# Three output chunks at once in the first batch's second layer, and the weight loads of the next batch at its end

## The chip, the cores and the metric

The kernel runs on one core of one Trainium2 chip. The metric is device time in microseconds (us) of one execution. The core has five engines that run their own instruction lists side by side and wait for each other by semaphores: TensorE (PE in the profile; PEld is its weight load), VectorE (DVE), ScalarE (ACT), GpSimd (POOL), and SyncE (SP), which here only issues DMA transfers.

## The reference

Eight batches of attention with normed queries and keys, then a two-layer block over all 3584 rows:

```python
q_n = q / sqrt(mean(q*q, -1) + 1e-6) * g_q        # q, k, v: (8, 12, 448, 64), float32
k_n = k / sqrt(mean(k*k, -1) + 1e-6) * g_k
attn = softmax(q_n @ k_n.T / sqrt(64)) @ v        # softmax over the keys
x = attn.transpose(0, 2, 1, 3).reshape(8 * 448, 768)
h = x @ w_in                                      # w_in: (768, 2048)
out = ((h - tanh(h)) @ w_out).astype(float32)     # w_out: (2048, 768)
```

`w_in` and `w_out` come in as float64, two 32-bit words for each number; the kernel rounds them to float32 itself.

## The kernel before

**Attention** is cut into 48 steps, one for each batch and pair of heads (numbered `s`; six steps to a batch). Each step's q and k blocks (`qk_nat`) and v block (`v_nat`) are loaded by SP, the squares are summed and turned into a factor `rr`, q and k are multiplied by it, transposed on TensorE (L467, L471), multiplied to scores (L569), put through the exponential on ScalarE (L575), and multiplied with v (L635, L623, L677). The sums for the softmax are products with ones (L700, in `totals`), and `totals` takes their reciprocal on VectorE (L705). Results of TensorE lie in banks of two pools: `sc` with five banks for attention and `mm` with three for the two layers; each pool is handed out in turn, so a bank is free again only when its last reader is done. For two steps (s = 11 and 12, in `visit`) `totals` takes a bank of `mm`.

**The two layers** are written as a Python generator, `mlp()`. It yields after each matmul, and the attention slots draw so many of them between their own parts. So the two kinds of work are interleaved in one list on TensorE, in an order fixed when the program is built. For the first two batches the generator gives, in order, `hidden(0)`, `project_first(0)`, `hidden(1)`, `project(1)`.

- `hidden(b)` is the first layer of batch b by a scheme of seven products in place of eight: four sets (`j` = 0 to 3) of seven products `p`, in the order 1, 5, 6, 2, 3, 7, 4. A product is 12 matmul records at L857 and takes about 2.27 us. After a product, `use(p, bank)` takes it from its bank: a copy by ScalarE for p=1 (L924), sums by VectorE for p=5, 6, 7, 3, 4 (L926, L928, L932 and L933, L936, L940), a tanh and a difference for p=2 (`shrink`, L904 and L905); the other differences are queued in `late["todo"]` and come some products later, on GpSimd. The three `mm` banks take turns, with p=2, 3 and 7 added into the banks of 1, 5 and 6.
- `project_first(0)` is the plain second layer of batch 0: six output chunks of 128 columns, each a chain of 16 matmuls (`f` = 0 to 15) of 448 columns at L1339, one chunk after the other (the right half of `w_out` first). At a chunk's end ScalarE copies the bank (L1345), and `store` transposes it on VectorE (L966) and queues its four DMAs (L971) in `late["out"]`, which `step_out` issues later.

**The weights** come in 32 pieces, 0 to 15 of `w_in` and 16 to 31 of `w_out`. A piece is loaded raw by SP (`weight_load`), and rounded in three stages: ScalarE (L71, L72), VectorE (L78, L79, L82), GpSimd (L92). Three raw buffers serve all pieces from the eighth on, and `place_free` lets a load be issued only when the piece three before it is through. `weight(to)` rounds pieces up to number `to`. In `hidden(0)` the list `due` gives `to` for each of the 28 products; in `project_first` a formula in `m` does, for the first three chunks. Four pieces of `w_in` make the eight operands of one set, by sums of VectorE in `combine` (L357), and `keep_step` writes the seven that are needed to a scratch tensor in DRAM (L388) for the later batches.

**The ring.** After `w_in` is used, its memory is a ring of six places (`SLOTS`), handed out in turn by `ring_slot`. `combine_w_out(f)` (L381 to L384) puts sums of `w_out` in two places, from where `keep_factors` writes them to DRAM; the DMAs wait in `late["keep"]` until the next such step. Then the ring serves `ring_load(to)`: it loads the operands of the next batches' layers up to number `to` from DRAM by SP (L427 in the first layer). `hidden(1)` uses one such load of 384 KB for each product.

In `project_first` the order before is, by matmul number `m` from 0 to 95:

| m | what is put in the lists ahead of the matmul |
|---|---|
| 0 to 47 | `weight(...)`, 8 pieces in all |
| 48, 49 | the last two pieces of `w_out` to DRAM |
| 52, 56, ... 80 | `combine_w_out(0)` to `(7)`, with the DMAs of the one before |
| 84 | two ring loads, then the last DMAs of `w_out` |
| 86 | two more ring loads |
| each chunk's middle | the stores of the chunk before (two `step_out`) |

The other ring loads are issued in `hidden(1)`, where places come free. In `hidden(1)` the attention slot also loads `qk_nat` in a changed form (L497): its squares are summed by ScalarE (L501, tile `sum_T`) and VectorE (L508, tile `rr_mine`), between the sums of the products in VectorE's list.

SP issues all DMAs of the kernel in one list, in the order in which the program was written. The framework puts in the semaphore waits.

Of the kernel before, what the change touches and what calls it, by code (L numbers as in the profile page):

```python
# [147 lines left out]
def bounded_path(tc, ctx, q, k, v, moe_w_in, moe_w_out, out, g_col, ident, ones, half_ones, neg_half, early):  # L148
# [66 lines left out]
    def mm_bank():  # L215
        return bank_of("mm")
# [170 lines left out]
    def keep_factors(n, count, f, src):  # L387
        nc.sync.dma_start(  # L388
# [28 lines left out]
            ring_steps += [(first, 2, p, part) for p in outer for part in (1, 2, 3, 4, 0)]  # L417
    ring_tiles = {}

    def ring_load(to):  # L420

        for n in range(len(ring_tiles), min(to, len(ring_steps))):
            b, layer, j, p = ring_steps[n]
            t = ring_tiles[ring_steps[n]] = ring_slot()
            if layer == 0:
                assert kept[1] > j
                nc.sync.dma_start(out=t[:, : 2 * HALF], in_=w_in_dram[j, p])  # L427
            elif layer == 2 and p == 0:
                nc.sync.dma_start(out=t, in_=w_out_dram[:, BLOCKS[j], HC - 1].rearrange("p f d -> p (f d)"))
            elif layer == 2:  # L430
                n = min(2 * HB, 7 * HB - 2 * (p - 1) * HB)
                at = 2 * (p - 1) * HB
                nc.sync.dma_start(out=t[:, :n], in_=inner_dram[j][:, at : at + n])
            else:
                nc.sync.dma_start(out=t, in_=w_out_dram[:, BLOCKS[p], j].rearrange("p f d -> p (f d)"))


    normed, turned, probs, sums, whole, xT, tt = {}, {}, {}, {}, {}, {}, {}
# [208 lines left out]
    def visit(s, av):  # L647

        wave(*half_values(s, 2, av, True))
        for c in range(2):  # L650
            v0, v1 = half_values(s, c, av, False)
            if has(s + 1):
                (s0, exp0), (s1, exp1) = scores(s + 1, c, True)
                wave(s0, v1)
                exp0()
                wave(v0, s1)
                exp1()
            else:
# [158 lines left out]
    assert len(due) == 7 * SETS and due[-1] == CF + HF  # L817

    def part(name):
        if name == "th" and "blocks" in late:  # L820
# [60 lines left out]
    def hidden(b):  # L881

        if b < PAIRED or b % 2 == 0:
            g = gp.tile([P, CF, S], F32, name="gT")
        else:
            g = late["second"].tile([P, CF, S], F32, name="g2")
        late["g"] = g
        if b >= PAIRED:
            late.setdefault("us", {})
            late["pair_g"] = [g, None] if b % 2 == 0 else [late["pair_g"][0], g]  # L890
        single = b and b < PAIRED
        t2 = late["tg"].tile([P, 3, HF, HS], F32, name="tg") if single else None
        late["t"] = t2
        x = [xT.pop((b, c)) for c in range(CD)]
        t = [tt.pop((b, i)) for i in (0, 1, 3)]
        low, high = slice(0, HS), slice(HS, S)
        moving = {
            1: lambda c: x[c][:, low], 2: lambda c: x[c + HC][:, low], 3: lambda c: x[c + HC][:, high],
            4: lambda c: t[2][:, c], 5: lambda c: t[0][:, c], 6: lambda c: t[1][:, c], 7: lambda c: x[c][:, high],
        }  # L900

        def shrink(rows, cols, h, eng):
            th = part("th")
            nc.scalar.activation(th, h, AF.Tanh, bias=0.0, scale=1.0)  # L904
            eng.tensor_tensor(out=g[:, rows, cols], in0=h, in1=th, op=ALU.subtract)  # L905

        def done_with(j):
            up, down = slice(2 * j, 2 * j + 2), slice(HF + 2 * j, HF + 2 * j + 2)
            s1, s2, s5 = part("s1"), part("s2"), part("s5")

            def factors():

                g11, g12, _, g22 = (g[:, r, c] for r in (up, down) for c in (low, high))
                f1, f2 = (t2[:, i, up] for i in range(2))
                nc.vector.tensor_tensor(out=f1, in0=g12, in1=g11, op=ALU.subtract)
                nc.vector.tensor_tensor(out=f2, in0=g22, in1=f1, op=ALU.subtract)
                nc.gpsimd.tensor_tensor(out=g12, in0=g22, in1=g12, op=ALU.subtract)

            def use(p, bank):
                v = view(bank)  # L920
                if b >= PAIRED:
                    beside_hidden(b, j, p)
                if p == 1:
                    nc.scalar.copy(out=s1, in_=v)  # L924
                elif p == 5:
                    nc.vector.tensor_tensor(out=s5, in0=v, in1=s1, op=ALU.add)  # L926
                elif p == 6:
                    nc.vector.tensor_tensor(out=s2, in0=v, in1=s1, op=ALU.add)  # L928
                elif p == 2:
                    shrink(up, low, v, nc.vector)  # L930
                elif p == 7:
                    nc.vector.tensor_tensor(out=s5, in0=v, in1=s5, op=ALU.add)  # L932
                    nc.vector.tensor_tensor(out=s1, in0=v, in1=s1, op=ALU.add)  # L933
# [375 lines left out]
    def project_first(b):  # L1309
# [4 lines left out]
        late["todo"] = []  # L1314
        keep_step(0, SETS - 1)
        took = 4 * S / ENGINE_NS
        for m in range(CD * CF):
            k, f = m // CF, m % CF
            n = (k + HC) % CD
            if f == 0:  # L1320
                bank = mm_bank()
            if f == CF // 2:
                step_out(2)
            if k < HC:
                weight(CF + HF + HF * (m + 1) // (HC * CF))
            elif m < HC * CF + 2:
                keep_w_out(PIECES - 2 + m - HC * CF)
            elif (m - HC * CF) % 4 == 0 and m - HC * CF <= 4 * HF:
                for fn in late["keep"]:
                    fn()  # L1330
                late["keep"] = []
                combine_w_out((m - HC * CF) // 4 - 1)
            elif m == CD * CF - 12:
                ring_load(2)
                for fn in late["keep"]:
                    fn()
            elif m == CD * CF - 10:
                ring_load(4)
            nc.tensor.matmul(  # L1339
                bank[:, :S], lhsT=w_out_row(f, n // HC)[:, n % HC * P : (n % HC + 1) * P], rhs=g[:, f, :],  # L1340
                start=(f == 0), stop=(f == CF - 1),
            )
            if f == CF - 1:
                y = part("s2").rearrange("p f s -> p (f s)")
                nc.scalar.copy(out=y, in_=bank[:, :S])  # L1345
                store(b, n, y)
            yield took
        wp_stack.close()
        late["blocks"] = pool("blocks", bufs=1)
# [530 lines left out]
```

## Time and profile before

Three runs took 1344.74, 1344.65 and 1343.43 us, median 1344.65. The profiled execution is one more run.

| what | value |
|---|---|
| profiled execution, whole | 1342.53 us |
| its span, from first to last instruction | 1340.70 us |
| mean granted clock of TensorE | 0.998 of full |
| ScalarE / VectorE / GpSimd busy | 42% / 72% / 59% |
| `project_first(0)`, L1339, from first to last matmul | 176.25 to 268.5 us, with attention between |
| first record of `hidden(1)` | 274.46 us |

How to read it: one line of a timeline is one instruction or a run of like ones: start, length, engine, source line, operation, tiles written and read, and in brackets how long the engine had been idle before it and what ended that (the engine, tile and line whose result came last). TensorE's matmuls overlap, so a run of records is read by its start and end, not by adding their lengths. The names `w_f`, `w_out` and `w_in` of tiles are the ring (as operands of `w_in` and later loads), the rounded `w_out`, and the scratch in DRAM.

### The profile page before, as it was taken

To read this page: it belongs to the slowest core of one execution; us is meant where nothing else is said; L and a number is where in the kernel's file an instruction comes from. 1 tells how busy PE (TensorE), PEld (TensorE's weight loads), DVE (VectorE), ACT (ScalarE), POOL (GpSimd) and SP (SyncE) were. 2 spreads that over 40 slices of the span, in tenths; PEclk is the share of its full clock that TensorE was granted. 3 is DMA by queue.
4 is the path that set the end of the run, shared out by engine and by line. 5 is a ranking of instruction groups with operands and counts; after the bars stand their busy time and mean duration, and the time that the engine had idled before them with its cause. 6 is when DMAs were issued, how large, how long until landed. Compare 5 with 4: busy or idle time off the path is not lost.

```text
span 1340.7 us, 29301 instructions
## 1 busy us (share of the span) xinstructions
PE 1311.5 (98%) x11368; PEld 1033.4 (77%) x11368; DVE 969.5 (72%) x1410; ACT 568.1 (42%) x1328; POOL 795.0 (59%) x591
## 2 busy tenths in 40 slices
PE   7989999999999999999999999999999999999997
PEld 3467854488998888688878788779887888799986
DVE  4999978867765767688888576768888667634455
ACT  7856654244343454445322445454512254311102
POOL 4766776348846256726698245944699244812771
PEclk9999999999999999999999999999999999999999
DMA  7779889889999766476655867466745776466544
GB/s 169 183 214 262 265 260 231 250 278 279 340 284 287 181 160 180 112 186 155 171 149 136 201 162 183 117 170 165 181 132 145 150 201 161 118 161 172 170 142 102
DMA packets 364759, 253.53 MB, mean 189 GB/s; under 512 B 273028, under 2 KB 303300, under 8 KB 364612
## 3 DMA queue, kind: packets, MB, share of 16 engines
q1 hardware_dynamic: 364608, 251.57, 69.1%
q8 instruction: 92, 1.51, 0.5%
q14 instruction: 55, 0.45, 0.1%
q10 hardware_dynamic: 4, 0.00, 0.0%
HBM read 205.23 MB, written 46.27 MB: 188 GB/s over the span
## 4 chain that ended last, share of the span: by engine, by line
PE 83%; DVE 7%; POOL 4%; DMA 2%; SPq 2%; issue 2%; ACT 1%; DVEq 0%; ACTq 0%; POOLq 0%
PE mm L857 38%; PE mm L1142 21%; PE sc L569 9%; PE sc L635 6%; PE mm L1339 5%; POOL u L1099 3%; PE sc L623 1%; POOL rr_mine L523 1%; PE sc L677 1%; DVE w_out L357 1%; PE mm L677 1%; SPq L497 1%; DVE rs L705 1%; DMA w_f<-w_inner 1%; DVE w_out L82 0%
## 5 line engine op out<-in xcount | busy, mean ns | idle before, releaser
L857 PE MATMUL mm<-xT,w_f 128*128 128x224 f32 x1296 | 263.5, 353 | 0.8 <-DVE xT L767 0.8
L857 PEld LDWEIGHTS mm<-xT,w_f 128*128 128x128 f32 x1296 | 244.8, 190 | 5.5 <-issue 4.2
L569 PE MATMUL sc<-qT,kT 64*32 64x448 f32 (+1 forms) x3072 | 215.6, 499 | 2.7 <-ACT p_last L575 2.1
L857 PE MATMUL mm<-tt,w_f 128*128 128x224 f32 x1044 | 212.6, 355 | 0.2 <-DMA w_f<-w_in 0.2
L857 PEld LDWEIGHTS mm<-tt,w_f 128*128 128x128 f32 x1044 | 195.8, 190 | 15.9 <-issue 15.4
L523 POOL TENSOR_TENSOR rr_mine<-rr_mine,neg_half 128x28 f32<-128x28 f32 x33 | 162.2, 4915 | 2.7
L762 DVE TENSOR_TENSOR xT<-xT,sc 128x448 f32<-128x448 f32 x34 | 21.0, 618 | 165.8 <-PE sc L569 114.8
L1142 PE MATMUL mm<-u,w_f 128*128 128x224 f32 x672 | 137.2, 354 | 1.0 <-POOL u L1099 0.5
L905 POOL TENSOR_TENSOR gT<-s,th 128x448 f32<-128x448 f32 x44 | 57.8, 1313 | 132.2 <-ACT th L904 128.7
L1142 PE MATMUL mm<-gT,w_f 128*128 128x224 f32 (+3 forms) x512 | 132.0, 412 | 1.2 <-DVE acc L1149 0.9
L1142 PEld LDWEIGHTS mm<-u,w_f 128*128 128x128 f32 x672 | 126.1, 190 | 8.0 <-POOL u L1099 3.6
L569 PEld LDWEIGHTS sc<-qT,kT 64*32 64x32 f32 x3072 | 72.4, 106 | 68.1 <-issue 49.2
L1142 PEld LDWEIGHTS mm<-gT,w_f 128*128 128x128 f32 x512 | 93.9, 190 | 34.3 <-issue 32.0
L635 PE MATMUL sc<-p,v_nat 64*32 64x448 f32 x1184 | 116.9, 536 | 0.0
L1142 PE MATMUL mm<-g,w_f 128*128 128x224 f32 (+1 forms) x360 | 98.9, 428 | 0.0
L575 ACT ACTIVATE p<-sc 128x448 f32<-128x448 f32 x132 | 71.9, 545 | 50.3 <-PE sc L569 37.4
L905 POOL TENSOR_TENSOR g<-s,th 128x448 f32<-128x448 f32 x24 | 30.3, 1264 | 105.1 <-ACT th L904 105.1
L1142 PEld LDWEIGHTS mm<-g,w_f 128*128 128x128 f32 x360 | 67.9, 190 | 26.5 <-issue 26.0
L729 ACT COPY sum_g<-sum 32x14 f32<-32x14 f32 x280 | 56.3, 201 | 72.0 <-DVE sum L721 66.3
L1339 PE MATMUL mm<-gT,w_out 128*128 128x448 f32 x192 | 74.0, 542 | 0.0
L145 POOL TENSOR_TENSOR rr<-rr,neg_half 112x8 f32<-112x8 f32 (+1 forms) x30 | 49.8, 1689 | 35.5 <-DVE rr L144 35.0
L1099 POOL TENSOR_TENSOR u<-gT 128x448 f32<-128x448 f32 x48 | 63.5, 1342 | 11.1 <-PE mm L1142 11.1
(206 smaller groups left out, 2465.8 us busy)
## 6 DMA issues: line engine op xcount, KB each, us to landing
w_f<-w_in SPq DMA_DIRECT2D x196, 384.0 KB, 3.5
w_f<-w_inner SPq DMA_DIRECT2D x63, 512.0 KB, 3.7
w_f<-w_out SPq DMA_DIRECT2D x42, 512.0 KB, 3.9
w_raw<-in_moe_w_out_dram SPq DMA_DIRECT2D x16, 768.0 KB, 5.4
w_in<-w_out SPq DMA_DIRECT2D x21, 384.0 KB, 5.3
qk_nat<-in_q_dram SPq DMA_DIRECT2D x132, 56.0 KB, 2.6
qk_nat<-in_k_dram SPq DMA_DIRECT2D x132, 56.0 KB, 2.4
g<-w_out SPq DMA_DIRECT2D x14, 512.0 KB, 5.4
```

The lines of the kernel that those rows point to most:

```text
L145: nc.gpsimd.tensor_tensor(out=r, in0=r, in1=neg_half[:rows], op=ALU.pow)
L523: nc.gpsimd.tensor_tensor(out=mine, in0=mine, in1=neg_half[:, :1].to_broadcast([P, 2 * NJ]), op=ALU.pow)
L569: nc.tensor.matmul(tiles[h][i * BL : (i + 1) * BL, :n], lhsT=kT[r, c * P + at : c * P + at + BL], rhs=qT[r, first : first + n], start=True ...
L575: nc.scalar.activation(p[:, h, c if c < 2 else 0, :], tiles[h][:, :n], AF.Exp, scale=1.0 if rr is None else rr[:, 0, 2 * c + h : 2 * c + h ...
L635: nc.tensor.matmul(av[g][i * BL : (i + 1) * BL, :S], lhsT=v_nat[keys, h, c, m * BL : (m + 1) * BL], rhs=p[keys, h], start=first, stop=True ...
L677: nc.tensor.matmul(av[n][r : r + BL, :HS], lhsT=v_nat[:, h, c, m * BL : (m + 1) * BL], rhs=p[c][:, h, n * HS : (n + 1) * HS], start=False, ...
L729: nc.scalar.copy(out=acc[h * BL : (h + 1) * BL, g], in_=part[g * BL : (g + 1) * BL, h * NJ : (h + 1) * NJ])
L857: nc.tensor.matmul(bank[:, f * HS : (f + 1) * HS], lhsT=w[:, c * width + f, :], rhs=moving[p](c), start=(first and f == 0 and c == 0), sto ...
L905: eng.tensor_tensor(out=g[:, rows, cols], in0=h, in1=th, op=ALU.subtract)
L1099: nc.gpsimd.tensor_tensor(out=u[:, half], in0=a[:, half], in1=z[:, half], op=ALU.subtract)
L1142: nc.tensor.matmul(bank[:, :n], lhsT=w(i), rhs=mv, start=(first and i == 0), stop=(i == len(moving) - 1), skip_group_check=not first,)
L1339: nc.tensor.matmul(bank[:, :S], lhsT=w_out_row(f, n // HC)[:, n % HC * P : (n % HC + 1) * P], rhs=g[:, f, :], start=(f == 0), stop=(f == C ...
```

## The change

`project_first` runs three output chunks at once: `f` is the outer loop and three chunks the inner, in two groups of 48 matmuls, with a bank of `mm` for each of the three. Three copies, transposes and sets of stores come together at the end of each group. The pace of the weights changes: `due` asks for pieces 8 to 22 evenly over the 28 products of `hidden(0)` (before 8 to 16 over the first half and 16 to 24 over the second), and `behind` for the other ten over 58 matmuls of `project_first`. `combine_w_out` comes six matmuls later, and its last two f are written to DRAM in single factors. All six ring places are loaded at the end of `project_first`, ahead of the last group's stores. Three further ring loads are issued by ScalarE in the first set of `hidden(1)`, after its copy of p=1, after p=6 and after its tanh of p=2. `totals` in `visit` takes a bank of `sc`.

```diff
@@ combine_w_out @@
-        late["keep"].append(lambda: [keep_factors(3 + 2 * i, 2, f, t[i]) for i in range(2)])
+        if f < HF - 2:
+            late["keep"].append(lambda: [keep_factors(3 + 2 * i, 2, f, t[i]) for i in range(2)])
+            return
+        late["keep"].append(lambda: [keep_factors(3 + n, 1, f, s) for n, s in enumerate((s3, s1, s2, s4))])
@@ ring_load: every nc.sync.dma_start becomes queue.dma_start @@
-    def ring_load(to):
+    def ring_load(to, queue=nc.sync):
@@ visit @@
-            totals(s, mm_bank())
+            totals(s, sc_bank())
@@ pace of the weights @@
-    due = [EARLY + (CF - EARLY) * (m + 1) // (7 * SETS // 2) for m in range(7 * SETS // 2)]
-    due += [CF + HF * (m + 1) // (7 * SETS // 2) for m in range(7 * SETS // 2)]
+    SOON_OUT, LAST_OUT = HF - 2, 58
+    due = [EARLY + (CF - EARLY + SOON_OUT) * max(m - 1, 0) // (7 * SETS - 2) for m in range(7 * SETS)]
+    behind = [min(PIECES, CF + SOON_OUT + (PIECES - CF - SOON_OUT) * (m + 1) // LAST_OUT) for m in range(CD * CF)]
@@ use, in hidden @@
                 if p == 1:
                     nc.scalar.copy(out=s1, in_=v)
+                    if single and j == 0:
+                        ring_load(SLOTS + 1, nc.scalar)
...
                 elif p == 6:
                     nc.vector.tensor_tensor(out=s2, in0=v, in1=s1, op=ALU.add)
+                    if single and j == 0:
+                        ring_load(SLOTS + 2, nc.scalar)
                 elif p == 2:
                     shrink(up, low, v, nc.vector)
+                    if single and j == 0:
+                        ring_load(SLOTS + 3, nc.scalar)
@@ project_first, the loop after @@
+        combined = [0]
+        def keep_combined(to):
+            for f in range(combined[0], min(to, HF)):
+                for fn in late["keep"]:
+                    fn()
+                late["keep"] = []
+                combine_w_out(f)
+                combined[0] = f + 1
+        for m in range(CD * CF):
+            k, f, i = m // (HC * CF), m % (HC * CF) // HC, m % HC
+            n = (1 - k) * HC + i
+            if m % 4 == 3:
+                step_out()
+            weight(behind[m])
+            if f == 0:
+                bank = [] if i == 0 else bank
+                bank.append(mm_bank())
+            if LAST_OUT <= m < LAST_OUT + 2:
+                keep_w_out(PIECES - 2 + m - LAST_OUT)
+            if m >= LAST_OUT - 4:
+                keep_combined((m - LAST_OUT + 4) // 4)
+            if m == CD * CF - 6:
+                for fn in late["keep"]:
+                    fn()
+                late["keep"] = []
+            if m == CD * CF - 4:
+                ring_load(2)
+            elif m == CD * CF - 2:
+                ring_load(SLOTS)
             nc.tensor.matmul(
+                bank[i][:, :S], lhsT=w_out_row(f, n // HC)[:, n % HC * P : (n % HC + 1) * P], rhs=g[:, f, :],
                 start=(f == 0), stop=(f == CF - 1),
             )
             if f == CF - 1:
+                y = part(("s2", "s5", "s1")[i]).rearrange("p f s -> p (f s)")
+                nc.scalar.copy(out=y, in_=bank[i][:, :S])
+                store(b, n, y, part("s2").rearrange("p f s -> p (f s)") if i == 2 else None)
             yield took
```

More of the change, by code (lines that the diff above doesn't have):

```diff
@@ L426, in ring_load @@
                 assert kept[1] > j
-                nc.sync.dma_start(out=t[:, : 2 * HALF], in_=w_in_dram[j, p])
+                queue.dma_start(out=t[:, : 2 * HALF], in_=w_in_dram[j, p])
             elif layer == 2 and p == 0:
-                nc.sync.dma_start(out=t, in_=w_out_dram[:, BLOCKS[j], HC - 1].rearrange("p f d -> p (f d)"))
+                queue.dma_start(out=t, in_=w_out_dram[:, BLOCKS[j], HC - 1].rearrange("p f d -> p (f d)"))
             elif layer == 2:
@@ L432, in ring_load @@
                 at = 2 * (p - 1) * HB
-                nc.sync.dma_start(out=t[:, :n], in_=inner_dram[j][:, at : at + n])
+                queue.dma_start(out=t[:, :n], in_=inner_dram[j][:, at : at + n])
             else:
-                nc.sync.dma_start(out=t, in_=w_out_dram[:, BLOCKS[p], j].rearrange("p f d -> p (f d)"))
+                queue.dma_start(out=t, in_=w_out_dram[:, BLOCKS[p], j].rearrange("p f d -> p (f d)"))
     normed, turned, probs, sums, whole, xT, tt = {}, {}, {}, {}, {}, {}, {}
@@ L812, in bounded_path @@
     late = {}
-    due = [EARLY + (CF - EARLY) * (m + 1) // (7 * SETS // 2) for m in range(7 * SETS // 2)]
-    due += [CF + HF * (m + 1) // (7 * SETS // 2) for m in range(7 * SETS // 2)]
-    assert len(due) == 7 * SETS and due[-1] == CF + HF
+    SOON_OUT, LAST_OUT = HF - 2, 58
+    due = [EARLY + (CF - EARLY + SOON_OUT) * max(m - 1, 0) // (7 * SETS - 2) for m in range(7 * SETS)]
+    behind = [min(PIECES, CF + SOON_OUT + (PIECES - CF - SOON_OUT) * (m + 1) // LAST_OUT) for m in range(CD * CF)]
+    assert due[-1] == CF + SOON_OUT and due[7 * (SETS - 1) - 1] > CF
     def part(name):
@@ L1316, in project_first @@
         took = 4 * S / ENGINE_NS
[L1317 to L1328, printed above, removed]
+        combined = [0]
+        def keep_combined(to):
+            for f in range(combined[0], min(to, HF)):
                 for fn in late["keep"]:
@@ L1331, in project_first @@
                 late["keep"] = []
-                combine_w_out((m - HC * CF) // 4 - 1)
-            elif m == CD * CF - 12:
-                ring_load(2)
+                combine_w_out(f)
[14 more added lines that the diff above has]
+            if m == CD * CF - 6:
                 for fn in late["keep"]:
                     fn()
-            elif m == CD * CF - 10:
-                ring_load(4)
+                late["keep"] = []
[3 more added lines that the diff above has]
+                ring_load(SLOTS)
             nc.tensor.matmul(
-                bank[:, :S], lhsT=w_out_row(f, n // HC)[:, n % HC * P : (n % HC + 1) * P], rhs=g[:, f, :],
+                bank[i][:, :S], lhsT=w_out_row(f, n // HC)[:, n % HC * P : (n % HC + 1) * P], rhs=g[:, f, :],
                 start=(f == 0), stop=(f == CF - 1),
@@ L1343, in project_first @@
             if f == CF - 1:
-                y = part("s2").rearrange("p f s -> p (f s)")
-                nc.scalar.copy(out=y, in_=bank[:, :S])
-                store(b, n, y)
+                y = part(("s2", "s5", "s1")[i]).rearrange("p f s -> p (f s)")
+                nc.scalar.copy(out=y, in_=bank[i][:, :S])
+                store(b, n, y, part("s2").rearrange("p f s -> p (f s)") if i == 2 else None)
             yield took
```

## The prediction

> **What bounds the kernel now.** I read the page's busy shares first, then the waits of TensorE over the span, then its timeline beside VectorE's around each wait, then the ends of the first batch's second layer.
>
> ```profile
> span 1340.7 us, 29301 instructions
> PE 1311.5 (98%) x11368; PEld 1033.4 (77%) x11368; DVE 969.5 (72%) x1410; ACT 568.1 (42%) x1328; POOL 795.0 (59%) x591
> ...
> L1339 PE MATMUL mm<-gT,w_out 128*128 128x448 f32 x192 | 74.0, 542 | 0.0
> ```
> TensorE is busy 98% of the span. The second layer of the first batch (L1339) has no idle time ahead of it in 192 records, so its 96 products can't be made faster by feeding them better.
>
> ```profile
> PE mm L467 <- DVE rr L143: 5.2, 1, 5.2
> PE sc L467 <- DVE rs L705: 3.9, 2, 2.3
> PE mm L857 <- DVE s L926: 2.5, 1, 2.5
> PE sc L569 <- ACT p_last L575: 2.1, 1, 2.1
> PE mm L857 <- DVE xT L767: 0.8, 1, 0.8
> ```
> Columns: engine, place, what it waited for: us in total, times, longest. This is nearly all that any change can win. Two of the entries, L705 and L926, lie in the first batch's first layer, which the change repaces. The 5.2 is at the start and 2.1 of L575 is not near the change.
>
> ```profile
> 83.77 0.66 PE L467 MATMUL sc<-ident,qk_nat 128*128 128x128 f32 x4 [1.57 <-DVE rs L705]
> 91.15 2.81 PE L857 MATMUL mm<-xT,w_out 128*128 128x224 f32 x8 [2.54 <-DVE s L926]
> 114.43 3.95 PE L857 MATMUL mm<-xT,w_out 128*128 128x224 f32 x20
> 120.70 0.66 PE L467 MATMUL sc<-ident,qk_nat 128*128 128x128 f32 x4 [2.32 <-DVE rs L705]
> ```
> Three waits of 1.57, 2.54 and 2.32 us, all for VectorE: one is for a sum that frees a bank, two for a reciprocal whose bank the transposes (L467) need. What VectorE does ahead of the last:
>
> ```profile
> 107.01 1.07 DVE L78 TENSOR_SCALAR w_f<-w_f 128x768 f32<-128x768 f32 x1
> 108.11 1.25 DVE L79 TENSOR_SCALAR w_f<-w_f 128x768 int32<-128x768 int32 x1
> 109.40 1.78 DVE L82 SCALAR_TENSOR_TENSOR w_f<-w_raw,w_f 128x768 int32<-128x768 int32 x1
> 111.10 2.64 DVE L357 TENSOR_TENSOR w_f<-w_f 128x768 f32<-128x768 f32 x2
> 118.23 0.95 DVE L357 TENSOR_TENSOR w_f<-w_f 128x768 f32<-128x768 f32 x1
> 119.09 1.55 DVE L705 RECIPROCAL rs<-sc 128x224 f32<-128x224 f32 x1
> ```
> It rounds weight pieces and forms sums of them; the reciprocal comes after all of that, though its operand is done at 111.2 (the L700 sums of TensorE).
>
> **The change, part by part.** (1) *The pace of the weights in the first layer.* In the changed program's own order, VectorE's list is the same up to and with the L926 sum of 90.48 us, so the waits at 83.77 and 91.15 stay. Behind it one rounding of a piece (three instructions, 0.83 + 1.25 + 0.96 = 3.0 us at 91.01) and the two L357 sums of 111.10 (2.64) leave the path to the reductions L143; another piece (0.55 + 0.56 + 0.96 = 2.1) and the L357 of 118.23 (0.95) that stood between the L926 of 115.64 and the reciprocal come after it. Then L926 begins when its product ends (about 115) and the reciprocal follows it: 115 + 0.6 + 1.55 = about 117.2, against 118.38 (120.70 less 2.32), when TensorE wants the bank. The other input of that turn, the normed n on ScalarE, ended at 117.39 + 2.02 = 119.41, behind POOL's rr at 115.66; in the new order POOL does the L905 product (1.13) ahead of the L92 pair, so rr starts up to 1.1 us sooner and n ends by about 118.6, when it is wanted at 118.9 (TensorE's L471 comes 0.49 us behind L467). So the 2.32 goes; if n does not move, 119.41 - 118.87 = 0.5 of it stays. Gain: 2.2, bounds 1.8 and 2.5. Nothing of TensorE is idle from there to 440 us, so nothing else can be won. Two pieces less in the layer means two more in the second; same work, rounded there every 5.6 us as before (8 pieces over 48 products of 0.765 us, now 10 over 58), about 3 us of VectorE each.
>
> (2) *Three chunks at once.* 96 matmuls with two records each stay, at the mean of 542 ns; 0. Attention parts stand between products 47 and 48 as before; the copies of the first two banks (0.53 each on ScalarE) end while the third chunk's last products run, so the third is where one copy stood. Cover of all three: the attention behind each group (268.51 to 274.46, 6 us, at the second). If that cover fell short, one copy, 0.5 us, would be seen.
>
> (3) *totals in an sc bank*, two sites: 16 + 8 + 8 records as before; 0. The bank pool is less full in one place and fuller in another; bound 0 to 1.57 by the one L705 wait it resembles.
>
> (4) *Combining six products later, and single-factor stores for the last two f.* Four more DMAs on SP at about 0.5 us of issue each: 2 us, and 4.6 us of delay (six products), so the last ends at about 264 to 266, where before the queue was at the stores of 263.51. VectorE's sums (L381 to L384) are the same in number.
>
> (5) *Ring loads ahead of the stores.* Six loads at 264 to 269 on SP. Before, the transfers between 255 and 275 were at the ceiling:
>
> ```profile
> 255.00:260.00 5.00, 5.00 (x15) 2.55 (x14) 4.32 (x10) 0.53 (x1) 0.00 (x0) 1.00 1.15 346
> 260.00:265.00 5.00, 5.00 (x14) 2.47 (x13) 4.83 (x8) 0.00 (x0) 0.43 (x1) 1.00 1.04 299
> 265.00:270.00 5.00, 5.00 (x50) 2.31 (x56) 0.95 (x3) 1.26 (x3) 2.81 (x2) 1.00 1.13 326
> ...
> w_f<-w_in SPq DMA_DIRECT2D x14, 384.0 KB, 5.4
> ```
> (stretch, TensorE, its loads, VectorE, ScalarE, POOL, clock, DMA share, GB/s; then the issues of 255 to 300, the last number from issue to landing.) First load 264.5 + 5.4 = about 270; hidden(1) begins at 274.46 less the 2.2 gained, 272.2. Margin 2 us, so 0, bounds 0 and 3 (a stall if the combining is 5 us late). The stores land later; their buffers are not wanted again before the next stores.
>
> (6) *Three loads issued by ScalarE.* The issue itself takes about 0.5 us each on an engine that is idle 6.28 us ahead of its tanh at 284.68; 0. The Trainium skill (DMA: Bandwidth & Descriptors, Issuing engines are not separate DMA queues) says that such loads share the same DMA engines and that another issuing engine saves only issue time; by it there is no bandwidth to win, and the sum would be the same.
>
> But the loads add a wait. In the changed program's waits each DMA waits, in order of the program over both queues, for the eighth before it. SP's last load of qk_nat thus waits until ScalarE's third ring load has landed, and that one is issued behind the tanh of product p=2 of hidden(1). Before, that path was short:
>
> ```profile
> 282.21 6.97 PE L857 MATMUL mm<-xT,w_f 128*128 128x224 f32 x36
> 284.68 0.54 ACT L904 ACTIVATE th<-mm 128x448 f32<-128x448 f32 x1 [6.28 <-PE mm L857]
> 287.29 0.95 ACT L501 ACTIVATE sum_T<-qk_nat 128x896 f32<-128x896 f32 x1
> 288.27 1.08 DVE L508 TENSOR_REDUCE rr_mine<-sum_T 128x28 f32<-128x896 f32 x1 [0.70 <-ACT sum_T L501]
> 289.28 0.61 DVE L932 TENSOR_TENSOR s<-mm,s 128x448 f32<-128x448 f32 x1
> 289.81 0.61 DVE L933 TENSOR_TENSOR s<-mm,s 128x448 f32<-128x448 f32 x1
> ```
> Behind L508 on VectorE stand the two sums of product p=7, whose bank the second product of the next set wants. From the end of p=2: tanh 0.54, issue 0.5, landing 3.5 (the page's median for these loads), qk_nat's issue 0.4 and landing 2.4 (page), L501 0.95, L508 1.08, two sums 1.2: 10.6 us. TensorE meanwhile has p=3, 7, 4 and the next p=1: four products at 2.27 = 9.1. Stall 1.5. Bounds: below, 0 where the load lands in 2 us; above, landing 5.4 and qk_nat 4.0 (v_nat's median there): 14.1 - 9.1 = 5.0. I take 1.5, the end that the lighter traffic at 280 to 285 (0.67 busy) is nearer to. Also queued behind ScalarE's sum are the copies L729 and the tanh of p=7.
>
> Sum: -2.2 + 1.5 = -0.7. The profiled execution took 1342.53 us (span 1340.70 and 1.83 around it), 2.1 below the median of the runs, 1344.65; so 1341.8 by the profile and, rounded, **1344.0** by the median.
>
> *The clock.* The granted clock was 0.67 in 90 to 95 us, behind the 2.54 of idle, and 1.00 in 120 to 125, behind the 2.32. So a stall over 2.5 costs about 5 x 0.33 = 1.6 more. The Trainium skill (TensorE: Matmul & The Clock Gate, HAM oscillation — how this bites in real kernels) warns of idle gaps over some 3.4 us only; by that the stall of 1.5, and one of 2.5 as well, would cost nothing more, and the sum is the same.
>
> **The rivals.** *Hidden.* qk_nat lands before VectorE needs it (light traffic, landing 2): -2.2, 1342.4 or, with the wait of 91.15 also easing (2.5 and 1.6 of clock at stake, though VectorE's order up to it is unchanged), down to 1340. Against it: the load can't start before the tanh. *ScalarE's loads couple the queues hard.* The upper bound above, 5.0 of stall and 1.6 of clock, less 2.2: +4.4, 1349; it decides from a stall of 4.9 (the gain and 2.7), that is, from 9.5 us for the two landings together, against 5.9 in the forecast. For it: 5.4 for these loads between 255 and 300; against it: before, 0.67 busy at 280 to 285, but the change moves stores there. *Late start.* Combining late, first ring load after 272.2: 1 to 3 us, with the gain +0 to +1, and +2.5 to +4 with forecast's stall. *No effect.* The turn still waits, for n or another piece: gain 0.5, with the stall +1.1, 1345.7.
>
> **How the numbers follow.** Forecast (-1.8 to +1.2: 1342.9 to 1345.9) 0.36, no effect 0.08, hidden 0.25, hard coupling 0.19, late start 0.12. About 0.2% (2.7 us) is what a measurement tells from no change. Faster by over that: most of hidden with easing, and the runs' scatter of 1.3, 0.22. Slower: coupling and most of late start, 0.28. Same 0.50. Range 1340.8 to 1349.6, leaving about 1 in 10 on either side; the forecast's own is 1342.9 to 1345.9.
>
> **What would show it.** The L705 wait (now line 708) loses its 2.3 and keeps the 1.6 at 84; the wait at 91 stays. In hidden(1), TensorE idles ahead of the second product of j=1 with VectorE's sums 942 or 943 as releaser, ScalarE's line 504 waits for a DMA of qk_nat, SP shows a wait for a w_f load. Line 1358 keeps 542 ns with no idle. I am wrong if idle appears ahead of hidden(1), if its landing is over 5, or if the 120 us wait remains.

## The result, and the profile after

The changed kernel takes 1347.34 us (median of 22 runs, 1343.67 to 1352.07), the kernel before 1343.39 us (median of 22, 1341.50 to 1348.57). The ratio is 1.0027, 95% interval 1.0018 to 1.0036: slower by 3.6 us by the ratio (3.95 between the medians). The forecast was 0.7 us faster, which is no change clear of noise. The profiled execution of the changed kernel took 1348.88 us (span 1347.0), 1.5 above its median, and that of before 1342.53, 0.9 below its own. So the two traces show 6.3 us of difference, 2.4 more than the medians.

Of TensorE's waits in the changed kernel, those that bear on the change (engine, place, what it waited for: us in total, times, longest):

```profile
PE mm L861 <- DVE s L943: 5.9, 1, 5.9
PE mm L861 <- DVE s L932: 2.5, 1, 2.5
PE sc L470 <- DVE rs L708: 1.6, 1, 1.6
PE mm L861 <- DVE gT L909: 1.4, 1, 1.4
PE mm L861 <- DMA w_f<-w_in: 0.2, 1, 0.2
```

The reciprocal's entry is down from 3.9 in two waits to 1.6 in one, and a wait of 5.9 us for the sum of line 943 is new; so is the one of 1.4 for a tanh's difference (line 909). TensorE's timeline (start, length, engine, line, operation; in brackets the idle time before it and what ended it):

```profile
119.18 3.21 PE L861 MATMUL mm<-xT,w_out 128*128 128x224 f32 x16
271.10 1.78 PE L861 MATMUL mm<-xT,w_f 128*128 128x224 f32 x8
287.93 2.43 PE L861 MATMUL mm<-xT,w_f 128*128 128x224 f32 x12
296.26 6.10 PE L861 MATMUL mm<-tt,w_f 128*128 128x224 f32 x20 [5.89 <-DVE s L943]
350.27 4.78 PE L861 MATMUL mm<-xT,w_f 128*128 128x224 f32 x24 [1.43 <-DVE gT L909]
```

Set beside the same records of before, these and three more starts give the account of the two traces:

| place | before | after | after less before |
|---|---|---|---|
| behind the turn at 120 us | 121.58 | 119.18 | -2.4 |
| first record of hidden(1) | 274.46 | 271.10 | -3.4 |
| second product of its set 1 | 293.56 | 296.26 | +2.7 |
| products 2, 3 and 7 of set 1 (36 records) | 303.72 | 308.58 | +4.9 |
| first records of the next layer (gT, w_f) | 350.23 | 357.15 | +6.9 |
| span | 1340.7 | 1347.0 | +6.3 |

The first layer's gain came, and larger than forecast. Then 5.89 us of idle and a slow clock behind it (the 20 records took 6.10 us, before 3.95) took 8 us, and another 2 went by 350 us. Windows of the changed kernel there (stretch, TensorE, its loads, VectorE, ScalarE, POOL, granted clock, DMA share, GB/s):

```profile
285.00:290.00 5.00, 5.00 (x28) 5.00 (x27) 0.00 (x0) 0.80 (x4) 2.49 (x2) 1.00 1.10 266
290.00:295.00 5.00, 0.37 (x2) 0.02 (x1) 0.95 (x1) 1.81 (x6) 0.00 (x0) 0.86 0.90 267
295.00:300.00 5.00, 3.74 (x10) 3.42 (x11) 3.94 (x8) 3.40 (x9) 4.40 (x4) 0.50 0.95 383
```

From 290 to 295 us the engines are nearly idle (ScalarE's 1.81 us is the longest) and the transfers go on. Whose transfers, SyncE's and ScalarE's timelines show (SPq and ACTq are the lists that issue DMAs):

```profile
270.54 0.97 SPq L117 DMA_DIRECT2D v_nat<-in_v_dram  x2
273.04 6.97 SPq L981 DMA_DIRECT2D out_dram<-th  x8
280.12 1.05 SPq L1038 DMA_DIRECT2D g<-w_out  x2
281.27 2.90 SPq L981 DMA_DIRECT2D out_dram<-s  x4
284.21 3.80 SPq L500 DMA_DIRECT2D qk_nat<-in_q_dram  x4
288.05 2.05 SPq L500 DMA_DIRECT2D qk_nat<-in_k_dram  x4
```

```profile
281.32 0.54 ACT L908 ACTIVATE th<-mm 128x448 f32<-128x448 f32 x1 [6.28 <-PE mm L861]
285.36 0.33 ACTq L430 DMA_DIRECT2D w_f<-w_in  x1
285.73 0.88 ACT L732 COPY sum_g<-sum 32x14 f32<-32x14 f32 x4 [3.86 <-DMA g<-w_out]
293.07 0.95 ACT L504 ACTIVATE sum_T<-qk_nat 128x896 f32<-128x896 f32 x1 [6.47 <-DMA w_f<-w_in]
```

Eight stores held SyncE for 7 us, so the loads of g went out at 280.12. Not all of the 7 us is the stores' own: SyncE's waits show 2.4 us ahead of one of them for a ring load to land, and 0.7 ahead of a load of qk_nat for a load of g:

```profile
SPq L981 <- DMA w_f<-w_in: 2.6, 2, 2.4
SPq L500 <- DMA g<-w_out: 0.7, 1, 0.7
```

ScalarE's third ring load was ready behind the tanh at 281.9 and stood until 285.36 for the first g load to land. It did not hold up qk_nat: it landed 3.5 us later, at 288.9, and the last load of qk_nat went out behind the others of its list at 289.6 and landed 3.3 us later, at 292.9. ScalarE's sum (L504) began at 293.07; before, it ran at 287.29 and waited for nothing. (The line names the load `w_f<-w_in` as what ended the wait. The two loads share a semaphore, so the profile can name one for the other; the landing at 292.9 is that of qk_nat.) The loads of qk_nat went out at 284.2 to 290.1. In the kernel before they went out 7 us sooner, with four stores between the start of hidden(1) and them, and not twelve:

```profile
273.22 3.74 SPq L971 DMA_DIRECT2D out_dram<-th  x4
277.01 4.10 SPq L497 DMA_DIRECT2D qk_nat<-in_q_dram  x4
281.15 2.04 SPq L497 DMA_DIRECT2D qk_nat<-in_k_dram  x4
```

### The profile page after: what moved, and what is told of

The parts are those of the page before. It is cut to its first block, busy times and chain, and to the rows that moved or that the text cites. A ratio compares the mean times of both kernels' runs of the same rounds, so it can differ in the third digit from the quotient of the medians.

```text
span 1347.0 us, 29298 instructions
## 1 busy us (share of the span) xinstructions
PE 1313.1 (97%) x11368; PEld 1034.6 (77%) x11368; DVE 969.3 (72%) x1410; ACT 568.3 (42%) x1328; POOL 789.7 (59%) x591
## 4 chain that ended last, share of the span: by engine, by line
PE 85%; DVE 5%; POOL 4%; DMA 2%; issue 1%; ACT 1%; SPq 1%; DVEq 0%; ACTq 0%; POOLq 0%
PE mm L861 40%; PE mm L1152 20%; PE sc L572 9%; PE sc L638 6%; PE mm L1358 5%; POOL u L1109 2%; PE sc L626 1%; PE sc L680 1%; POOL rr_mine L526 1%; DMA w_f<-w_in 1%; PE mm L680 1%; DVE w_out L357 1%; DVE rows L616 0%; PE sc L703 0%; DVE rows L609 0%
```

## The experiments

Each run's time is the median beside runs of the kernel before on the same chip; the ratio is to those. A trace is of one execution, up to 3.6 us from the median of its kernel's runs (eight stores less: 1346.31 against 1343.32; earlier and staggered: 1349.37 against 1345.73; qk_nat first: 1344.79 against 1347.33). So the waits in a trace say where time went, and the medians how much.

**SyncE issues the three loads.** Does it matter that ScalarE issues them?

```diff
-                        ring_load(SLOTS + 1, nc.scalar)
+                        ring_load(SLOTS + 1)
```
and the same for the other two.

> The three ring loads of hidden(1) are issued by SyncE instead of ScalarE, at the same places of the program. Queue theory (each DMA waits for the eighth before it, whoever issues it; the third load waits for a load of g that lands at 285.3 us, and the last load of qk_nat waits for the third load): nothing of that goes, TensorE's wait for VectorE's sum ahead of the second product of set 1 stays at 4 to 7 us, time 1346 to 1349. ScalarE theory (the load is late because it stands behind the tanh in ScalarE's list): the wait falls to 2 us or less, time 1342 or less.

1346.03 us, ratio 1.0014 (1.0002 to 1.0025). Neither was right about the place: the wait for the sum is gone, and a wait for weights has come for it.

```profile
286.18 2.51 PE L861 MATMUL mm<-tt,w_f 128*128 128x224 f32 x12 [1.28 <-DMA w_f<-w_in]
292.97 4.82 PE L861 MATMUL mm<-xT,w_f 128*128 128x224 f32 x12 [4.29 <-DMA w_f<-w_in]
```

SyncE put the loads of set 1 behind those of qk_nat (three at 289.30), so the same late list now held up a weight: 5.6 us in two waits. So the loss does not come from ScalarE as the issuer. Whether a part of it does is open: the interval overlaps the changed kernel's (1.0018 to 1.0036), and the middle is half as far from 1.

**The loads of qk_nat first.** They are issued at the slot's start, ahead of the stores.

```diff
         scaled = rows and not first
+        if first:
+            load_blocks(s + 3)
...
-                (following, lambda: add_third(s + 1)), (first, lambda: load_blocks(s + 3)),
+                (following, lambda: add_third(s + 1)),
```

> The eight loads of qk_nat for the slot are issued at its start, ahead of the twelve stores and of the three loads of ScalarE; all else as in the changed kernel. If the late qk_nat is the whole of the loss: the wait of 5.9 us for the sum falls under 0.5, the slow clock after it goes too, and the 3.4 us gained up to the start of hidden(1) stay: 3 to 4 us under the kernel before, 1339.5 to 1341. Rival (the transfers are at their ceiling, whatever the order): the wait moves to the weight loads of set 1 or to the stores, time 1344 or more.

1347.33 us, 1.0027 (1.0016 to 1.0038): no gain, as the rival had it. The waits for the sum are gone, and 7 us of others have come:

```profile
PE mm L861 <- DMA w_f<-w_in: 5.4, 5, 1.5
PE mm L861 <- DVE gT L909: 1.6, 1, 1.6
```

The second is for a difference behind a tanh whose buffer (`th`) was still being stored, since the stores now came last: ScalarE's timeline has the tanh at 284.59, idle for 11.17 us until a store was done. Whichever of stores, qk_nat and weights goes last is late.

**The third load left to SyncE's usual place.**

```diff
                     shrink(up, low, v, nc.vector)
-                    if single and j == 0:
-                        ring_load(SLOTS + 3, nc.scalar)
```

> ScalarE's third load is left to SyncE's usual place, behind the loads of qk_nat. ScalarE theory (the last load of qk_nat waits for that load alone): the wait for the sum falls to 2 us or less, time 1343 to 1344. Stores theory (the loads of qk_nat are late because twelve stores and the loads of g stand ahead of them, and the last one then waits for the last store, issued at 284.2 us and landing 5 us later): the sum is still 4 to 5 us late, and the load of product p=5 itself comes some 4 us later than before; time 1346 to 1350.

1347.07 us, 1.0022 (1.0010 to 1.0034). The wait is 3.34 us and the slow clock costs 2.8 more (20 records in 6.75 us), between the two expectations in size, and the time is that of the stores theory. Without that load qk_nat is still late: its last loads go out by 289.2, and ScalarE's sum begins at 290.99, 3.7 us later than in the kernel before.

```profile
294.18 6.75 PE L861 MATMUL mm<-tt,w_f 128*128 128x224 f32 x20 [3.34 <-DVE s L941]
```

**The pace alone**, in the kernel before.

```diff
-    due = [EARLY + (CF - EARLY) * (m + 1) // (7 * SETS // 2) for m in range(7 * SETS // 2)]
-    due += [CF + HF * (m + 1) // (7 * SETS // 2) for m in range(7 * SETS // 2)]
+    SOON_OUT = HF - 2
+    due = [EARLY + (CF - EARLY + SOON_OUT) * max(m - 1, 0) // (7 * SETS - 2) for m in range(7 * SETS)]
...
-                weight(CF + HF + HF * (m + 1) // (HC * CF))
+                weight(CF + SOON_OUT + (PIECES - CF - SOON_OUT) * (m + 1) // (HC * CF))
```

> The kernel before with the new pace of the weights in the first layer alone (22 pieces evenly over 28 products, the other ten over the first three chunks of the second layer). Pace theory: the wait of 2.3 us at 120 us goes, and most of the 3.4 us that the changed kernel is ahead at hidden(1): time 2.3 to 3.4 us under the kernel before. Rival (the bank of totals or the three chunks bring part of it, or the pieces are late in the second layer): less than 1.5 us under it, or a wait for a weight in the second layer.

1351.95 us, 1.0047 (1.0029 to 1.0066). Both halves of the question are answered. The second layer begins at 172.93 us, against 176.25 before: the pace alone brings the 3.3 us. But a chunk that runs alone wants eight pieces within 16 products, and gets them late:

```profile
172.93 6.28 PE L1338 MATMUL mm<-gT,w_out 128*128 128x448 f32 x16
184.23 1.02 PE L1338 MATMUL mm<-gT,w_out 128*128 128x448 f32 x2 [0.94 <-POOL w_out L92]
188.07 3.35 PE L1338 MATMUL mm<-gT,w_out 128*128 128x448 f32 x4 [1.54 <-POOL w_out L92]
280.77 1.78 PE L856 MATMUL mm<-xT,w_f 128*128 128x224 f32 x8
```

hidden(1) begins at 280.77, 9.7 us later than in the changed kernel. The waits for pieces are 2.7 us of that, and a wait for ScalarE's exponentials at 229 us is 1.8. Behind both the granted clock is below full (0.80 and 0.86 from 185 to 195, 0.90 and 0.76 from 225 to 235); the rest was not traced to a cause. In the changed kernel, with three chunks at once, TensorE waits for no piece there.

**The second group one chunk after the other**, with a quicker pace, so that eight stores leave earlier; and, in a second kernel, **the second group staggered** (three at once for six f, then chunk by chunk).

```diff
+            if k == 1 and m >= HC * (CF + TOGETHER):
+                left = m - HC * (CF + TOGETHER)
+                i, f = left // (CF - TOGETHER), TOGETHER + left % (CF - TOGETHER)
```
with `TOGETHER` 0 and 6; with 0, the last ten pieces are asked for over 46 matmuls.

> The second group of project_first goes one chunk after the other again (first group three at once), with the last pieces of w_out asked for over 46 matmuls instead of 58, since a single chunk needs them sooner; all else as in the changed kernel. Eight of its twelve stores then go out during project_first, four at the start of hidden(1), as before. Stores theory (twelve stores there, behind each other in a queue of eight, are the loss): TensorE's waits in hidden(1) for the sum, for weights and for gT fall under 1 us together, the gain of 3.4 us stays: 2.5 to 4 us under the kernel before. Rival (the six ring loads at the end and ScalarE's three are the loss): 4 us or more of waits in hidden(1), time 1 us or more over the kernel before.

> The second group goes three at once for six of its sixteen f, and then finishes chunk by chunk; pace and all else as in the changed kernel. Chunks end at matmuls 75, 85 and 95, so that eight stores go out before hidden(1). Stores theory: as for the second group in single chunks, 2.5 to 4 us under the kernel before, waits in hidden(1) under 1 us together. Rival (ring loads and ScalarE's loads): 1 us or more over it.

1349.76 us, 1.0051 (1.0038 to 1.0064), and 1348.24 us, 1.0025 (1.0011 to 1.0038): both missed. The first lost its time in the second layer (hidden(1) began at 276.90) and tells little on the stores. In the second the wait for the sum is gone as expected, but eight stores ahead of the ring loads made the first of these late:

```profile
273.91 3.36 PE L861 MATMUL mm<-xT,w_f 128*128 128x224 f32 x8 [2.63 <-DMA w_f<-w_in]
296.00 3.95 PE L861 MATMUL mm<-tt,w_f 128*128 128x224 f32 x20
```

**Eight stores less.** The first two chunks of the second group are not written (256 columns of batch 0 stay empty).

```diff
+                if k == 1 and i < 2:
+                    late["out"].pop()
```

> The changed kernel without the stores of the first two chunks of the second group of batch 0 (those 256 columns of its output are not written): eight DMAs of 56 KB less at the start of hidden(1), nothing else changed. Stores theory: SyncE comes to the loads of qk_nat 5 to 7 us sooner, the wait of 5.9 us for the sum goes, time 2.5 to 4 us under the kernel before. Rival (ScalarE's third load sets the time of the last load of qk_nat): it waits for a load of g, which also comes sooner, but still for the tanh of p=2: a wait of 1 to 2 us stays, time 1 to 2 us under the kernel before.

1343.32 us, 1.0000 (0.9984 to 1.0016): level with the kernel before, so the 3.6 us of the changed kernel's loss are gone, and no more than these. (Twelve runs spread from 1339.16 to 1350.82.) The third ring load still went out only at 284.72, here behind a load of qk_nat and not of g, and the wait for the sum is gone all the same. No wait is left between 268 and 300 us; 3.4 us for weights come between 300 and 350 in its profile. There the two kernels' lists of SyncE have met: TensorE entered hidden(1) 2.7 us ahead of before (271.73), yet the g loads go out at the same time. SyncE in this kernel, then in the kernel before:

```profile
322.02 0.80 SPq L1038 DMA_DIRECT2D g<-w_out  x2
```

```profile
322.02 0.80 SPq L1028 DMA_DIRECT2D g<-w_out  x2
```

So the stores explain the new wait, but not where the 3.4 us of gain goes once they are away.

**Combining and ring loads six matmuls earlier**, with the last ten pieces over 52 matmuls.

```diff
-    SOON_OUT, LAST_OUT = HF - 2, 58
+    SOON_OUT, LAST_OUT = HF - 2, 52
...
-            if m == CD * CF - 4:
+            if m == CD * CF - 10:
                 ring_load(2)
-            elif m == CD * CF - 2:
+            elif m == CD * CF - 8:
```

> The changed kernel with the last ten pieces asked for over 52 matmuls instead of 58, combine_w_out six matmuls earlier (as in the kernel before) and the ring loads at matmuls 86 and 88 instead of 92 and 94. Queue theory: the w_out DMAs and ring loads clear SyncE's list some 3 to 4 us sooner, the stores start with the transposes (about 270 us instead of 273) and the loads of qk_nat come 3 us sooner: the wait for the sum falls from 5.9 to 2 to 3.5 us and the slow clock after it goes, 3 to 4 us under the changed kernel, within 1 us of the kernel before. Rival (VectorE, 4.9 us busy of 5 there, can't round and combine sooner): the wait stays at 5 to 7 us, or a wait for a piece of w_out appears in the second layer; within 1.5 us of the changed kernel or over it.

1344.23 us, 0.9998 (0.9986 to 1.0011), where the changed kernel has 1.0027: the loss is gone, as the queue theory had it. Ring loads start at 261.81 (265.82 in the changed kernel), and the wait for the sum is 1.2. What is left is waits for weights, three of them between 317 and 347 us and one at 435, at the start of the third batch's first layer:

```profile
PE mm L861 <- DMA w_f<-w_in: 4.2, 4, 1.4
PE mm L861 <- DVE s L943: 1.2, 1, 1.2
```

Two runs then ask whether hidden(1) is bound by its transfers. **More loads in the kernel before**: 512 KB into unused room beside each pair of g loads.

```diff
+            nc.sync.dma_start(
+                out=room[:, 12 * HB : 14 * HB], in_=w_out_dram[:, BLOCKS[OUTER[i]], 2].rearrange("p f d -> p (f d)")
+            )
```

> The kernel before with one more load of 512 KB, into unused room, beside each of the seven pairs of g loads in hidden(1) and the layer behind it; nothing reads it. It asks whether that stretch has transfers to spare. Theory that it is bound by transfers as much as by TensorE (so that time gained ahead of it comes back as waits for weights): waits for w_f loads of 3 us or more, time 3 to 8 us over the kernel before (seven loads at 346 GB/s are 10.6 us of transfer). Rival (transfers have room, and only the crowd at the start of hidden(1) is late): waits for w_f under 1 us, time within 1 us of the kernel before.

1351.83 us, 1.0054 (1.0040 to 1.0068): seven loads cost 7 to 8 us, with waits for weights where the trace of the kernel before has none. Of the 5.5, 2.2 is in hidden(1), at 320 us, and 3.3 at 443, at the start of the third batch's first layer, behind the last of the extra loads.

```profile
PE mm L857 <- DMA w_f<-w_in: 5.5, 2, 3.3
PE mm L857 <- DMA w_f<-w_out: 1.2, 2, 0.8
```

**Combining earlier and staggering together.** The edits of both kernels above.

> Combining and ring loads six matmuls earlier together with the staggered end of the second group (three at once for six f, then chunk by chunk): eight of the twelve stores leave the start of hidden(1), and the ring loads stay at about 264 us. Queue theory: no wait for the sum, no wait for the first ring load, hidden(1) starts 2.5 to 3.4 us sooner than in the kernel before and reaches its second set without a wait; if the stretch behind is bound by transfers, 2 to 4 us of waits for w_f come there, and the time ends 0 to 2 us under the kernel before. Rival (nothing but the start of hidden(1) costs time): waits for w_f under 1 us, 3 us or more under the kernel before.

1345.73 us, 1.0010 (1.0001 to 1.0020), where combining earlier alone has 0.9998: missed. The stores that left the start of hidden(1) stood ahead of the v loads and of g instead, and a wait of 2.6 us for the sum and 4.3 for weights are there. Moving eight stores within a full list saves nothing.

**Half the bytes.** In the version that combines earlier, the ring loads of sets 1 to 3 of hidden(1) bring half of their columns; the other half of a place keeps older numbers, so this kernel leaves out part of the work.

```diff
-                queue.dma_start(out=t[:, : 2 * HALF], in_=w_in_dram[j, p])
+                w = HALF if b == 1 and j else 2 * HALF
+                queue.dma_start(out=t[:, :w], in_=w_in_dram[j, p][:, :w])
```

> The version with combining and ring loads six matmuls earlier, with the 21 ring loads of sets 1 to 3 of hidden(1) cut to half their columns (192 KB less each, 4 MB in all, the other half of a place keeps older numbers); the lists of all engines and the number of DMAs stay. Theory that hidden(1) is bound by bytes: the 4.2 us of waits for w_f fall under 1 us, and 2 us or more go against the version with whole loads, to 1 to 3 us under the kernel before. Rival (the queue of eight and SyncE's one list set the pace, not the bytes): waits for w_f of 3 us or more stay, within 1 us of the version with whole loads.

1339.49 us, 0.9963 (0.9949 to 0.9976): 5.2 us under the kernel before, more than expected, with the same list of instructions and DMAs. There is no wait from 268 to 400 us. The lead over the kernel before is 3.6 us at the start of hidden(1) (270.91) and still 3.4 at the start of the third batch's first layer. There TensorE waits 2.63 us for a whole load and begins at 429.90 (in the kernel before at 430.66, without a wait). The two traces end 2.8 us apart, the medians 5.2; the trace does not show the difference.

```profile
315.00:320.00 5.00, 5.00 (x28) 5.00 (x27) 3.78 (x9) 1.95 (x6) 5.00 (x4) 1.00 1.04 363
320.00:325.00 5.00, 5.00 (x103) 2.65 (x109) 0.96 (x2) 1.86 (x5) 4.75 (x6) 1.00 1.02 337
```

The same stretches with whole loads:

```profile
315.00:320.00 5.00, 4.54 (x25) 4.22 (x24) 4.76 (x10) 4.21 (x13) 3.55 (x4) 1.00 1.01 356
320.00:325.00 5.00, 4.31 (x23) 3.96 (x21) 2.94 (x5) 0.55 (x1) 4.38 (x4) 1.00 1.04 414
```

TensorE is busy all the time with the lighter loads. The DMA share of these two rows is as high as with whole loads, so a share near 1 alone does not tell a stretch that costs time from one that does not; over 315 to 330 us it is 0.93 against 1.03, with 277 against 391 GB/s. It is bytes, not the number of DMAs or the order in the list, that takes the gain in this stretch; that part of the loss is shown. What the bytes and the queue of eight (each DMA waits for the eighth before it) cost at the very start of hidden(1), each by itself, was not separated. No complete version beat the kernel before by more than its interval.

## Why the prediction was wrong

The sum was a gain of 2.2 less a stall of 1.5. Two of its steps failed. The stall's path was wrong: it ran from the tanh over ScalarE's third ring load to the last load of qk_nat and was to take 10.6 us; it took 14.9, because the loads of qk_nat were late in SyncE's own list, behind twelve stores and two loads of g that no term priced. And the gain ahead of hidden(1) was taken as kept to the end, where it was paid back.

- *The pace of the weights: right in kind, too small.* The turn's wait went, and the waits at 84 and 91 us stayed (1.57 and 2.54 again). More of VectorE's work left the way than was worked out: the sum that was to begin at about 115 began at 112.11, and the reciprocal ended at 114.2, not at 117.2. By the start of hidden(1) the gain was 3.4, not 2.2: one us more came between 121 and 183 us inside records that show no wait (16 score records at 130 us took 1.63 us before and 0.98 after, 16 at 161 us 1.29 and 0.98).
- *Three chunks at once, totals, four more DMAs: right.* Line 1358 has 542 ns and no idle. The first ring load went out at 265.82, not 264.5, and made no wait.
- *The new wait: right place, wrong path, wrong size.* TensorE idled ahead of the second product of set 1 for the sum of line 943, behind ScalarE's sum of qk_nat. From the start of the tanh to the end of the sum it took 14.9 us (281.32 to 296.20), not 10.6. The step that failed is that the last load of qk_nat waits until the third ring load has landed. By the prediction's terms that load of qk_nat would have landed at 288.7 (281.9 and issue 0.5, landing 3.5, issue 0.4, landing 2.4). The term "issue 0.5" was 3.5 us, since the ring load stood for the g load; but even so it had landed at 288.9, 0.7 us before the last load of qk_nat had its turn at 289.6, and that landed at 292.9. What set this turn was SyncE's list. Of the stores the prediction says only that they land later and that their buffers are not wanted again; that they put off the loads of qk_nat by 7 us (284.2, before 277.0) is in no term. Two runs agree: with the third load left out, 3.34 us of idle and 2.8 of slow clock remained; with eight stores less and the third load hardly sooner (284.72), the wait was gone.
- *The rivals.* Hard coupling had 5.0 of idle and 1.6 of clock; it came with 5.9 and 2.2. Its name was wrong: the third load had landed in time, and with SyncE as the issuer the wait moves to a weight. That its +4.4 came near the measured 3.6 to 3.95 is partly luck, since the gain was larger than it assumed and another loss came behind. The Trainium skill (DMA: Bandwidth & Descriptors, Issuing engines are not separate DMA queues), cited in the prediction, says that another issuing engine saves only the time of the issue; the run with SyncE's loads (1.0014 against 1.0027) shows no gain from ScalarE.
- *The clock: right in kind.* The price of 1.6 behind a long idle was 2.2.
- *What was missing.* The prediction took the gain as kept, because TensorE waits for nothing from 122 to 440 us in the kernel before. But no wait is not slack. A row that hints at it was in the prediction's own trace, the DMA share of 0.98 to 1.02 from 285 to 300 us:

```profile
285.00:290.00 5.00, 5.00 (x29) 5.00 (x28) 4.24 (x7) 3.43 (x12) 0.18 (x1) 1.00 0.98 373
290.00:295.00 5.00, 5.00 (x28) 5.00 (x27) 3.28 (x6) 3.02 (x8) 5.00 (x5) 1.00 1.02 410
295.00:300.00 5.00, 5.00 (x78) 3.41 (x84) 1.56 (x3) 1.12 (x3) 4.83 (x6) 1.00 1.01 358
```

Two runs show the limit: more bytes there cost 7 to 8 us, and with half the bytes of the ring loads a start 3.6 us sooner is still 3.4 us sooner at the start of the third batch's first layer. With whole loads it is paid back as waits for weights.

- *Slips in the working, which did not decide.* The pieces of the second layer come every 4.6 us by the figures in the prediction's bracket (48 x 0.765 over 8), not every 5.6; that figure holds only with the attention between the products. The stall of 4.9 needs 9.3 us for the two landings, not 9.5. The late start's +0 to +1 and +2.5 to +4 do not follow from its terms, which give -1.2 to +0.8 and, with the stall, +0.3 to +2.3 (up to 1.6 more with the clock). And the transfers were at their ceiling to 270 us, not to 275: the DMA share from 270 to 275 was 0.72.

## What to carry to other kernels

Where two resources are both near full, the trace shows waits on one only. Before counting a gain ahead of such a stretch, look at the other's share there and ask whether its list starts sooner too; a share near 1 is a reason to ask, and a run with fewer bytes answers. When a change moves transfers past each other, walk the whole list with its limit of transfers in flight, and price every element of the chain by what stands ahead of it, not by its own issue. Here an order that made one transfer early made another late, and only the run with fewer bytes gained.

## What the runs showed of the hardware

- Short idle times slowed TensorE unevenly. Behind 2.08 us in the kernel with eight stores less, 24 records took 6.46 us (otherwise 4.70); behind 2.63 in the staggered kernel, eight took 3.36 (1.78); behind 3.34 in the kernel without the third load, twenty took 6.75 (3.95). But behind the 2.32 at 120 us in the kernel before, and behind 2.63 both in the kernel that combines earlier and staggers (20 records in 4.05) and in the one with half the bytes (12 in 2.51, otherwise 2.43), next to nothing was slower. The Trainium skill (TensorE: Matmul & The Clock Gate, HAM oscillation — how this bites in real kernels) warns of gaps over 3.4 us; here 2.1 was enough at times. Its Part 1: The HAM clock gate says that the window runs freely and that the moment of the change depends on where in it the first matmul lands. That the same holds for a gap would fit these runs; none of them shows the window.
- Twelve stores of 56 KB, 0.7 MB in all, held SyncE's list for 9.9 us in the changed kernel, and six ring loads, 2.3 MB, for 4.7. One issue has a median near 0.5 us for both, so 5.7 us of the 9.9 is issuing (an estimate from these medians), and much of the rest is waiting for transfers ahead: 2.6 us for ring loads, 0.9 for a store. A transfer's place in the list is priced by its issues and by what stands ahead of it, not by its own bytes.
